# Cosformer attention with a token mixer on one core: a new order of all steps, narrow tiles for k'v and most transposes, eps on TensorE for 16 groups

## The chip, the core and the metric

The kernel runs on one core of a Trainium2 chip. The core has a matrix engine (TensorE, PE in the profile), three engines for elementwise work (VectorE or DVE, ScalarE or ACT, GpSimd or POOL) and a sync engine (SP), which here only issues DMAs. Each engine works through its own list of instructions in order and waits on semaphores where it needs another's result. The metric is the device time of one launch in microseconds, the median over runs.

## The reference

Two layers follow one another. The first is linear attention with a cosine weighting of positions, over 8 batches and 8 heads of 576 positions and 64 features; the second mixes tokens with weights that are made from the first layer's output.

```python
def phi(x, c, s):                       # c, s: cos and sin of pi/2 * pos/576
    r = np.maximum(x, 0.0)
    return np.concatenate([r * c, r * s], axis=-1)
q_p = phi(q, cos_w, sin_w); k_p = phi(k, cos_w, sin_w)
kv = einsum('bhsf,bhsd->bhfd', k_p, v);  z = sum(k_p, axis=2)
x = einsum('bhsf,bhfd->bhsd', q_p, kv) / (einsum('bhsf,bhf->bhs', q_p, z)[..., None] + 1e-06)
# x as [batch, 576, 512], heads side by side
wq = x @ w_q; wk = x @ w_k              # 512 -> 64
W_tok = einsum('bsd,btd->bst', wq, wk) / sqrt(64)
out = maximum(einsum('bst,btd->bsd', W_tok, x), 0.0) @ w_out
```

## The kernel before

The work is cut into 16 units H, each half of a batch's heads: batch H // 2, two pairs of heads. A suffix a or b on a step means the first or second pair alone. Everything is issued by one list of words, ORDER (line 26), which is walked from first to last (line 555): a word names a step, its number, after a colon its place in PSUM, and after an at sign its engine (A is ACT, V is DVE, G is POOL). Since each engine keeps the order in which it was given its instructions, this list sets the order on every engine and on SP. A scheduler does not move anything.

The steps of one unit H, in the order of its data:
- LK, LQ, LV (line 145): loads of k, q, v by SP, 128x576 f32 for each pair; five buffers of each, so a load for H waits for the steps that read H-5.
- RK, RQ (line 222, 225): relu of k and q to bf16 on any of the three engines. CV (line 229): cast of v to bf16. VS (line 232): product of the cast v with the table of cosines and sines (vtab), on DVE. VG (line 239): the same product straight from the loaded f32 v, on POOL, with no cast. Both write v2, of which there are two buffers, so H waits for KV of H-2.
- KV (line 268): k'v and z in PSUM. Wide, for units in KV_WIDE, it is 18 matmuls with 128 columns of weights and 260 streamed (line 275), half of whose output is not used; narrow it is 36 matmuls of 64x64 weights and 130 streamed (line 285). KE (line 304) copies it out.
- QT (line 290): transposes of relu(q); wide 9 of 128x128 (line 295), narrow 18 of 64x64 (line 301). QM (line 312): product with the table qtab, on DVE, from PSUM; two instructions after a wide QT, one after a narrow.
- N (line 332): numerators and denominators of group g = 2H + r, 20 matmuls. For g in EPS_PE two small matmuls with ones and split eps add eps to the denominators (line 348); for the others EP (line 354) adds it on ACT or DVE. RC (line 377) takes reciprocals, RJ (line 380) those of both groups of a unit at once. X (line 383): numerators times reciprocals, giving x, on DVE.
- XT or XR (lines 398, 409): transposes of x, ten of 128x128 or twenty of 64x64; XE (line 422) copies them out.

The steps of one batch b: WK and KW (x @ w_k and its copy), WQ and QW, KX and XK (wk' x and its copy), XA and XB (copies of 64x256 to the other half of the partitions, line 474), MX and ME (32 in all: wq times that, then the scaled relu). The steps of 36 rows of output: WO (line 504, four matmuls with w_out), OE (line 512, copy out to one of 16 output buffers), ST (line 518, the store, by SP). A store waits on SP for its OE, and what stands behind it on SP waits too; an OE waits for the store that last read its buffer. LW and CW load and cast the weights, TK to TB set up tables and constants, WU (line 544) issues matmuls on constants; its number gives how many and of which shape.

The list has no due times: what is placed ahead is issued ahead.

Of the kernel before, what the change touches and what calls it, by code (L numbers as in the profile page):

```python
# [31 lines left out]
RC6 LQ4a KX0:4 X6 RK2@A QT2:2 RC7 X7 CV5@A KV2:0 LK7a XK0@V LV4a QM2 XB0@G QW0@A XT3:6 LV4b KE2@A
RK5@A LK4a VS5a N5:0 WU5:2 LK4b N4:2 VS5b XE3@A RQ5@G LV7a EP5@V KV5:4 RC5 RC4 X5 XA0@A LV7b X4
QT5:6 KE5@A RQ4@G LQ7b MX0:0 QM5 XR2:2 ME0@A LQ7a QT4:4 XE2@A LQ6a N10:0 QM4 MX1:6 CV4@G LK7b EP10@A
ME1@A WK1:2 LV6b WQ1:3 RC10 KW1@A VS4 RK4@A LQ6b KX1:2 MX2:6 LW2 N11:4 XK1@V QW1@A ME2@A EP11@V
KV4:2 LK6b RC11 XA1@G X10 CV7a@A CV7b@G LK6a X11 MX5:6 MX4:0 KE4@A RQ7b@G LV6a RQ7a@A VS7 N8:2 N9:4
ME5@A LV8a ME4@A QT7:6 RK7@G LW3 EP8@V EP9@V RJ4 RQ6a@A XT5:0 X8 LW4 XB1@G XE5@A X9 KV7:2 LW5 RQ6b@G
QM7 LQ8b VG6b MX6:4 KE7@A XT4:0 LQ9b ME6@A MX7:2 XE4@V QT6:6 LV8b ME7@A N15:4 QM6 RK6a@A LQ8a MX3:2
N14:0 CV6a@G EP15@A RK6b@A WK2:6 LV9b ME3@A VS6a WQ2:7 LK8a KW2@A RC14 KV6:2 RC15 QW2@A LQ9a X14
CV8a@G KX2:7 LV9a KE6@A CW4@G X15 CW2@A N13:2 LK9a CW3@A CW5@V N12:0 EP13@V XR7:4 XK2@V LK8b WO8:6  # L40
RC13 XA2@A X13 EP12@A CV8b@G LK9b XE7@A WO2:7 RC12 VS8 LV11a WO7:2 CV9b@A RQ8a@G X12 OE8:0@A MX8:4
WO6:3 RQ8b@A RK8a@G LQ13a ME8@V OE7:1@A LQ11b XR6:0 RQ9a@G LQ10a WO1:6 CV9a@A XE6@V RQ9b@G LK11b
OE2:2@A WO4:2 LK11a VS9 OE6:3@A LQ11a RK8b@A QT9:0 RK9a@G OE1:4@A WK3:3 LV11b QM9 QT8:4 RK9b@G KW3@A
# [14 lines left out]
ME23@A OE20:10@V XR13:4 RQ15a@G MX22:6 RQ15b@V MX20:0 ST20 ME22@A WO15:2 VG15a ST17 XE13@V ME20@A  # L58
ST8 N28:6 OE18:9@V OE15:14@A ST9 N29:0 EP28@A QT15:4 RK15@A EP29@V RC28 WK6:3 RC29 X29 WO25:2 KW6@A
QM15 WQ6:3 OE25:15@A KV15:0 X28 QW6@A ST25 ST7 KX6:3 KE15@A ST15 N31:0 ST18 XR14:6 EP31@V N30:4 ST0  # L60
XE14@V WO23:2 EP30@A ST10 XK6@A RJ15 ST16 X30 XA6@G WO24:3 ST5 OE23:7@A XB6@G X31 WO26:2 OE24:0@A
# [537 lines left out]
```

## Time and profile before

| | before |
|---|---|
| median of 3 runs | 120.26 us (119.72 to 120.61) |
| profiled execution, first to last instruction | 117.9 us |
| granted TensorE clock, mean | 0.997 |
| moved by DMA | 39.38 MB, of it 29.62 read and 9.44 written in HBM |
| loads of k, q, v | 96 of 288 KB |
| stores | 36 of 256 KB |

The page gives the span of the profiled execution, 117.9 us; the launch and what lies around the span are in the runs' times alone, so the median stands 2.4 us above it. The page's busy time of an engine is a share of this span over stages with different limits. It is therefore read with the slices and the table of stretches, which show when an engine is full, and with the chain of waits, which shows what ended last. In the groups of instructions each row gives line, engine, operation, output and input, count, then busy time in us and the mean duration of one in ns, then idle time just ahead of them and what ended it. Durations of matmuls overlap, so busy time divided by the count is less than the mean.

### The profile page before, as it was taken

The page shows a single profiled execution, that of the slowest core. Times are in us where ns is not written, and L with a number is a line of the kernel's source. Part 1 is how long each engine was busy: PE and PEld are TensorE (multiplying, and loading weights), DVE is VectorE, ACT ScalarE, POOL GpSimd, SP SyncE. Part 2 cuts the span into 40 slices and gives each one's busy share as a digit, 9 for nine tenths or more (in the row PEclk, how much of TensorE's full clock was granted, in tenths as well). Part 3 has the DMA queues.
Part 4 walks back from the last instruction along what each step waited for, and adds up shares of the span by engine and source line. Part 5 has one row for each costly group of instructions (what it writes and reads, how often), then busy time and mean ns, then how long its engine had stood idle before and what let it go on. Part 6 is the DMA issues. An engine that isn't in the chain of part 4 may idle for free.

```text
span 117.9 us, 4967 instructions
## 1 busy us (share of the span) xinstructions
PE 96.3 (82%) x2109; PEld 65.3 (55%) x2109; DVE 91.0 (77%) x163; ACT 82.7 (70%) x146; POOL 64.8 (55%) x66
## 2 busy tenths in 40 slices
...
DMA  3999999999999999999999899786989456999874
GB/s 95 353 389 408 393 363 351 391 389 396 385 393 389 391 385 387 389 395 384 387 381 341 271 317 379 274 253 215 299 285 321 171 205 268 402 343 402 340 306 172
DMA packets 20662, 39.38 MB, mean 334 GB/s; under 512 B 3232, under 2 KB 3232, under 8 KB 20640
## 3 DMA queue, kind: packets, MB, share of 16 engines
...
HBM read 29.62 MB, written 9.44 MB: 331 GB/s over the span
## 4 chain that ended last, share of the span: by engine, by line
PE 46%; DMA 25%; DVE 9%; SPq 8%; ACT 4%; issue 3%; POOL 2%; POOLq 0%; DVEq 0%
PE ps L509 23%; DMA kraw<-in_k_dram 11%; DMA vraw<-in_v_dram 9%; SPq L145 8%; DMA qraw<-in_q_dram 5%; DVE qm L316 5%; PE ps L340 4%; PE ps L452 3%; PE ps L466 3%; PE ps L489 3%; PE ps L439 3%; PE ps L285 3%; PE ps L419 2%; PE ps L295 2%; POOL rq L205 2%
## 5 line engine op out<-in xcount | busy, mean ns | idle before, releaser
L248 POOL TENSOR_TENSOR v<-vraw,vtab 128x1152 bf16<-128x1152 f32 (+1 forms) x12 | 35.6, 2976 | 4.5 <-DVE qm L316 2.5
L509 PE MATMUL ps<-wow,mix 128*128 128x512 bf16 x144 | 34.6, 380 | 0.0
L393 DVE TENSOR_TENSOR x<-ps,rec 128x640 bf16<-128x640 f32 x32 | 25.4, 816 | 0.7
L209 ACT COPY o<-ps 128x512 f32<-128x512 f32 x25 | 14.6, 590 | 10.5 <-PE ps L509 9.2
L316 DVE TENSOR_TENSOR qm<-ps,qtab 128x1152 bf16<-128x1152 bf16 x28 | 19.7, 749 | 1.3 <-PE ps L295 1.2
L509 PEld LDWEIGHTS <-mix 128*128 128x128 bf16 x144 | 12.5, 98 | 14.5 <-issue 1.7
L295 PE MATMUL ps<-ident,rq 128*128 128x128 bf16 x126 | 10.3, 232 | 10.9 <-ACT rq L203 10.0
L234 DVE TENSOR_TENSOR v<-vb,vtab 128x2304 bf16<-128x2304 bf16 (+1 forms) x11 | 12.0, 1110 | 7.5 <-ACT vb L209 6.7
L500 ACT ACTIVATE mix<-ps 128x576 bf16<-128x576 f32 x23 | 14.5, 651 | 2.5 <-PE ps L489 2.3
L340 PE MATMUL ps<-kvs,qm 64*128 64x65 bf16 x640 | 14.0, 193 | 2.8 <-DVE qm L316 1.8
L340 PEld LDWEIGHTS <-qm 64*128 64x128 bf16 x640 | 12.6, 96 | 4.9 <-issue 3.3
L295 PEld LDWEIGHTS <-rq 128*128 128x128 bf16 x126 | 8.2, 104 | 12.5 <-issue 9.9
L203 ACT ACTIVATE rk<-kraw 128x1152 bf16<-128x1152 f32 (+1 forms) x14 | 13.9, 995 | 0.5 <-DMA kraw<-in_k_dram 0.3
L211 POOL TENSOR_SCALAR kx<-kx 64x256 bf16<-64x256 bf16 x10 | 4.0, 400 | 15.8 <-ACT kx L209 10.1
L205 POOL TENSOR_SCALAR rq<-qraw 128x576 bf16<-128x576 f32 (+1 forms) x13 | 10.1, 776 | 4.4 <-ACT rk L203 2.6
L211 POOL TENSOR_SCALAR vb<-vraw 128x576 bf16<-128x576 f32 (+1 forms) x7 | 5.7, 809 | 10.8 <-DMA vraw<-in_v_dram 9.5
L285 PE MATMUL ps<-v,rk 64*64 64x130 bf16 x432 | 9.1, 228 | 1.9 <-ACT mix L500 0.7
L209 ACT CAST kvs<-ps 128x260 bf16<-128x260 f32 (+1 forms) x15 | 6.5, 436 | 5.1 <-PE ps L285 3.8
L285 PEld LDWEIGHTS <-rk 64*64 64x64 bf16 x432 | 7.5, 112 | 4.3 <-ACT mix L500 1.3
L502 DVE TENSOR_SCALAR mix<-ps 128x576 bf16<-128x576 f32 x9 | 6.8, 753 | 3.3 <-PE ps L489 3.1
L213 DVE COPY xT<-ps 128x1280 bf16<-128x1280 bf16 (+1 forms) x9 | 7.3, 813 | 2.2 <-PE ps L419 2.0
L203 ACT ACTIVATE rq<-qraw 128x576 bf16<-128x576 f32 (+1 forms) x10 | 8.3, 830 | 0.9 <-DMA qraw<-in_q_dram 0.8
...
## 6 DMA issues: line engine op xcount, KB each, us to landing
kraw<-in_k_dram SPq DMA_DIRECT2D x32, 288.0 KB, 5.9
qraw<-in_q_dram SPq DMA_DIRECT2D x32, 288.0 KB, 5.9
vraw<-in_v_dram SPq DMA_DIRECT2D x32, 288.0 KB, 5.9
...
```

Of the source, the lines that this page charges most:

```text
L203: A.activation(dst, s, AF.Relu)
L205: eng.tensor_scalar(dst, s, FMAX, 0.0, op0=ALU.min, op1=ALU.max)
L209: A.copy(dst, s)
L234: V.tensor_mul(v2_b[H % NV2][:, part, :, :, 0:D], vb_b[H % NPREP][:, part].unsqueeze(3).to_broadcast([P, n, C, 2, D]), vtab.unsqueeze(1).t ...
L248: G.tensor_mul(dst[:, part, :, :, 0:D], s[:, part].unsqueeze(3).to_broadcast([P, n, C, 2, D]), vtab.unsqueeze(1).to_broadcast([P, n, C, 2, ...
L285: nc.tensor.matmul(kv_v[o, r, :], rk_of(H)[a, pr, c, :], v2_b[H % NV2][a, pr, c, :, 0:D + 1], start=(c == 0), stop=(c == C - 1))
L295: nc.tensor.transpose(qt_v[:, c, :], rq_b[H % NPREP][:, c, :, :], ident)
L316: V.tensor_mul(qm_b[H % NQM][:, :, r, 0:C, :], q_t[:, r].unsqueeze(1).to_broadcast([P, 2, C, H2]), qtab)
L340: nc.tensor.matmul(nv[:, pr, u, :], qm_b[H % NQM][a, s, r, 2 * u:2 * u + 2, :], kv_b[H % 2][a, r, pr if H in KV_WIDE else 0, s, 0:D + 1], ...
L393: V.tensor_tensor(x_b[b % NX][:, :, 4 * h:4 * h + 4, :].rearrange("p u (w r) d -> p r w u d", r=2)[:, r], nv[:, :, :, 0:D], rec(g).to_broa ...
L500: A.activation(dst, s, AF.Relu, scale=scale_moe)
L509: nc.tensor.matmul(o, mix_b[bp % 2][:, m, rt * P:(rt + 1) * P], wow[:, m, :], start=(m == 0), stop=(m == NDM - 1))
```

## The change

ORDER is replaced as a whole. All steps of the computation stay; on which engine they run, in what halves, and where they stand, changes throughout. Three settings change with it: all KV are narrow, all QT but those of units 0, 2 and 5 are narrow, and eps is added by TensorE in 16 groups instead of 5. Three of the four XT become XR. WU issues four matmuls at the start where one stood later. Units are taken in pairs in nearly the same sequence, but from unit 0 instead of 1.

Counts of the steps that go to an engine by choice (A, V, G as above; h is one pair of heads, f both or no halves):

| step | before | after |
|---|---|---|
| VS (V) | 6f 5h | 11h |
| VG (G) | 3f 9h | 2f 17h |
| CV | A 2f 4h, G 2f 5h | A 4h, G 4h, V 3h |
| RK | A 9f 5h, G 1f 4h, V 1f 1h | A 2f 17h, G 1f 4h, V 5h |
| RQ | A 3f 7h, G 3f 10h, V 1f 1h | A 2f 12h, G 1f 9h, V 2f 1h |
| EP | A 12, V 15 | A 5, V 11 |
| RC, RJ (V) | 24, 4 | 30, 1 |
| XE | A 7, V 9 | A 3, V 13 |
| KW | A 7, V 1 | A 3, V 5 |
| XK | A 4, V 4 | A 7, V 1 |
| XA and XB | A 6, G 10 | A 6, G 1, V 9 |
| ME | A 23, V 9 | A 28, V 4 |
| OE | A 25, V 11 | A 27, V 9 |
| CW | A 3, G 2, V 1 | G 6 |

KE, QW, X, QM, loads and stores keep their numbers and engines. The old list is cut below to its start, the part around KV11 and KV10, its last loads and its end; the new one is whole.

```diff
 ORDER = """
-LK1b TB TI LQ1a LQ0a TK LV1b TZ LV1a LK1a LQ1b TQ LQ0b LK0a RQ1a@G LV0a TW TV LV0b LK0b CV1@A LV3a
-LV3b VS1b RQ1b@A LQ3b VS1a T2 QT1:0 LQ3a RK1a@A RK1b@V RQ0@V LK3b KV1:2 QM1 LK3a QT0:4 KE1@A CV0@G
-LV2b RK0@A LW1 N2:2 VS0 N3:0 LQ2a LK2a VG3 QM0 KV0:6 LW0 KE0@A LV2a RC3 EP2@A X3 RQ3@A N0:6 N1:4
...
-WO9:5 LK12a X19 LK10b QT11:6 LQ13b OE9:7@A RQ10@G LV12b KV11:2 XA3@A QM11 XR8:0 LK12b KE11@A XR9:6
...
-KV10:2 OE3:9@V RQ12a@A QT13:6 OE12:10@A VG12 MX18:0 WO14:5 QM13 KE10@A ST12 ME18@A LK13b XR11:2
...
-RK13@A RJ12 QT14:0 X24 WO21:2 KW5@A X25 CV14a@G KV13:4 OE21:10@A QM14 CV14b@A WQ5:3 ST21 KE13@A
-KX5:2 LQ15b VS14 LQ15a XR12:4 XK5@A N27:0 ST3 XE12@A N26:6 LK15a RK14a@G WO20:2 RC26 EP27@V RC27
-XA5@G RK14b@A X27 WO19:4 XB5@G QW5@A VG15b X26 KV14:0 OE19:2@A MX21:6 KE14@A MX23:4 WO18:3 ME21@V
...
-XB7@G ST28 MX31:0 MX28:4 MX30:6 ME31@V ME28@A WO29:2 ME30@A OE27:7@V MX29:4 OE29:4@V WO30:0 ME29@A
-ST27 ST29 WO32:1 OE30:2@V WO33:4 ST30 OE32:9@V WO34:0 ST32 OE33:8@A WO35:1 ST33 OE34:7@V WO31:4 ST34
-OE35:4@A ST35 OE31:2@A ST31
+TB LV0b LQ0b LQ0a LV0a TI TQ CV0b@G LV1b LK0a LK0b WU17:0 TK TV LV1a TW CV0a@A T2 RQ0a@V LQ1a LQ1b
+TZ RK0a@A LK1b RQ0b@G LK1a CV1b@V LV2b LV2a LQ2a RQ1a@G VS0b LK2b LQ2b LK2a QT0:0 LQ3a RK0b@A CV1a@A
+LQ3b LW1 VS0a LW0 QM0 LV3a LV3b KV0:2 LK3b RQ1b@G VS1a LK3a LV4b LQ4b VG2 VS1b LQ5a KE0@A QT1:2 LQ5b
+LQ4a LV4a LK4a LV5a RK1b@A LK4b RQ3a@G LK5a QM1 N1:0 LK5b LV5b RK1a@A RC1 LW5 LW3 N0:4 RC0 KV1:6
+KE1@A LW2 CW1@G N2:6 EP2@A LW4 CW0@G RQ2a@A N3:2 X1 RQ2b@A X0 LQ6a RK2a@A LQ7b EP3@V XR0:4 RC2 LV6b
+LQ7a QT2:0 RK2b@A RC3 X3 X2 XR1:6 RQ3b@A LQ6b XE0@V KV2:4 KE2@A VG3a QM2 XE1@V LK6a LV7a LV6a CV3b@A
+VG4b QT3:2 WQ0:4 QM3 WK0:5 KW0@V RQ5@G LK6b N4:6 RK3b@A LV7b VG4a N5:2 VS3b KX0:5 XK0@A QW0@A EP5@V
+LK7a RK3a@V XA0@A RC5 RC4 X5 X4 KV3:0 MX1:4 MX0:2 KE3@A N6:0 ME0@A LK7b XR2:6 RC6 XB0@A ME1@A VG5a
+XE2@A X6 N7:2 RK5@G RC7 X7 MX3:0 RQ4@V LV8b XR3:2 QT5:6 ME3@A XE3@V QM5 LV8a CW3@G WK1:0 LQ8b KW1@A
+RK4@A LK8a QT4:2 WQ1:1 KX1:0 KV4:6 XK1@A QM4 XB1@V QW1@A CV5b@V VS5b LQ8a XA1@V KE4@A MX2:2 MX7:0
+MX6:4 N8:6 ME2@A ME6@A CW2@G ME7@A N9:2 LK8b KV5:4 LV9a KE5@A RC9 RC8 MX4:0 N11:4 X9 X8 ME4@A RC11
+N10:2 X11 LV9b CW4@G MX5:6 XR4:0 RC10 LQ9b CW5@G WO1:4 X10 ME5@A RQ7b@G CV6b@G XR5:2 RQ6a@A WO4:5
+RQ7a@G WO0:6 XE4@V LK9a LQ9a WO7:7 XE5@A LK9b VS6b QT7:2 LV10a OE4:0@V WQ2:5 RK6a@A OE1:1@A QM7
+CV6a@V VS6a RQ6b@G LV10b QT6:0 WO8:4 OE0:2@A WO2:6 RK6b@A KV6:2 QW2@A CV7b@A VG7a QM6 RK7a@V KE6@A
+OE7:3@A LV11b WK2:5 N12:2 RK7b@G VS7b N13:0 OE2:4@A KW2@A VG8b RC12 KV7:6 EP13@V LQ10a LQ10b X12
+OE8:5@A KE7@A RC13 X13 LK10b KX2:5 N14:6 N15:2 XR6:0 LV11a XK2@A RC15 XB2@A WO6:5 WO3:4 VG8a RC14
+RK8a@A RQ8@A XE6@V MX10:0 X14 QT8:6 RK8b@A VG9a X15 ME10@A LK11a LK10a KV8:2 OE3:6@A XT7:0 QM8 KE8@A
+XE7@V LK11b LQ11a VG9b MX11:2 LQ11b OE6:7@A N17:6 XA2@V N16:4 EP17@V LV13a ME11@A LV12a VG10a RQ9b@A
+RC16 LV12b WK3:0 RQ9a@A LQ13b RC17 WQ3:1 KW3@A MX8:2 X16 QT9:4 CV10b@G CV11b@G KX3:0 LQ12a X17
+RK9b@A QW3@A RK9a@V KV9:6 RK10b@G ME8@A MX9:2 LK12a XK3@A QM9 ME9@V XR8:0 KE9@A LQ13a LQ12b LK12b
+N19:6 XA3@V VG11a RC19 X19 XB3@A XE8@A WO10:4 N18:2 MX12:6 MX15:0 RC18 WO9:5 X18 VS11b LK13b XR9:2
+OE10:8@A WO12:4 XE9@V RK11b@G VS10b RQ10@A ME12@A ME15@A RQ11a@G MX13:0 OE9:9@A LV13b LK14a RK10a@V
+RK11a@A QT10:2 WK4:5 KV10:6 ME13@A KV11:0 OE12:10@A LK13a QM10 LQ15b KW4@V KE10@A N21:2 EP21@V RC21
+RQ11b@A MX14:6 VG13a QT11:4 KE11@A QM11 KX4:0 ME14@A WQ4:1 N20:6 XK4@A N22:4 ST9 X21 QW4@A N23:0
+VG12 RK13b@G RQ12a@A EP22@V WO13:2 LQ14a LV15b XB4@V RC20 EP23@V VG13b LV14a LK15b RJ11 X23 WO14:3
+LQ15a RK12a@V X22 OE13:11@A WO16:2 XR11:4 MX19:0 LV15a OE14:12@A XA4@A WO11:3 X20 OE16:13@A RQ12b@A
+XE11@V ME19@A XR10:6 MX18:4 RK12b@A ST12 RQ13@V QT12:0 ME18@A WO17:2 OE11:14@A XE10@V OE17:15@A
+WK5:4 QM12 RK13a@A QT13:6 RQ15b@G MX16:2 KV12:0 KW5@V LK14b KV13:4 ME16@A KE12@A MX17:2 QM13 N25:0
+N24:6 KE13@A EP24@V EP25@V N26:4 ME17@A RC24 KX5:2 RC25 X24 EP26@A XK5@A WQ5:3 VG15b RQ14a@A RK14a@A
+LK15a X25 RC26 LQ14b N27:6 LV14b X26 EP27@A QW5@A RC27 VG14a WO20:2 XA5@A WO5:0 OE20:9@A XR12:4
+MX21:2 RQ15a@A XB5@V X27 XE12@V ME21@A OE5:10@A XR13:6 VG15a WO15:1 XE13@V MX22:4 QT15:2 MX23:6
+ME23@V ST1 ME22@A VG14b WK6:0 WO18:4 ST10 ST14 RK15@A QM15 RK14b@A WO19:5 KW6@V ST11 ST7 RQ14b@A
+OE15:1@A OE19:8@A WO21:2 OE18:12@V OE21:14@A QT14:0 KV15:6 KV14:4 MX20:2 QM14 KE15@A KE14@V N30:6
+ST5 ST0 N31:0 EP30@V EP31@V RC30 N28:4 ME20@A ST3 RC31 WQ6:2 X30 X31 KX6:3 ST19 N29:6 QW6@A EP28@A
+WO24:2 WO23:0 EP29@A RC28 XK6@A X28 RC29 XR15:4 X29 ST2 OE24:3@A XB6@V XR14:6 XE15@V ST15 MX27:2
+ME27@A OE23:10@A ST16 ST21 XE14@V ST8 WO22:1 ST23 WO25:2 OE22:2@V XA6@V ST17 WK7:3 ST18 ST24
+OE25:6@A MX25:0 MX26:6 MX24:4 ME25@A ME24@A KW7@V WQ7:2 KX7:3 QW7@V ST13 ST6 XK7@V XA7@G XB7@V
+ME26@V WO26:4 MX31:2 WO29:5 ST25 MX29:6 ME31@A MX28:2 MX30:0 OE26:8@A ME30@A ME28@A WO27:4 ST20
+WO28:0 ME29@V ST4 WO30:1 WO34:2 ST26 OE27:4@V OE29:1@V OE28:13@V WO33:0 ST22 ST29 OE30:14@V ST28
+WO32:1 WO35:3 OE34:5@A ST30 OE35:10@A ST27 WO31:2 ST34 OE33:15@V OE31:12@A OE32:3@V ST33 ST32 ST35
+ST31
 """
...
     NRAW, NPREP, NV2, NQM, NX, NXT, NOUT = (5, 2, 2, 2, 2, 2, 16)
     XC = DM // 2
-    EPS_PE = (3, 4, 14, 16, 26)
+    EPS_PE = (0, 1, 4, 6, 7, 8, 9, 10, 11, 12, 14, 15, 16, 18, 19, 20)
     NUM_JOINT = ()
     WARM_COLS = 384
     VG_SPLIT = ()
-    QT_WIDE = (0, 1, 2, 3, 4, 5, 6, 7, 8, 9, 10, 11, 12, 14)
-    KV_WIDE = (2, 4, 5, 7)
+    QT_WIDE = (0, 2, 5)
+    KV_WIDE = ()
```

29 lines of the change are left out of this document (removed).

## The prediction

> **What bounds the kernel now.** I read the page first, then a table of stretches, the chain of waits and the order of the queues.
>
> ```profile
> span 117.9 us, 4967 instructions
> PE 96.3 (82%) x2109; PEld 65.3 (55%) x2109; DVE 91.0 (77%) x163; ACT 82.7 (70%) x146; POOL 64.8 (55%) x66
> ...
> DMA  3999999999999999999999899786989456999874
> GB/s 95 353 389 408 393 363 351 391 389 396 385 393 389 391 385 387 389 395 384 387 381 341 271 317 379 274 253 215 299 285 321 171 205 268 402 343 402 340 306 172
> ```
>
> Two engines are about equally full, and the transfers are full for the first half of the span. So no single share decides; the stretches do. The next fence is the table of stretches (length; busy time of PE, PEld, DVE, ACT, POOL; granted clock; DMA share; GB/s), cut at three points: the first DVE work on data, the issue of the last matmuls of KV10, and the end of PE.
>
> ```profile
> 8.60:64.50 55.90, 48.24 (x1136) 36.59 (x1140) 50.92 (x92) 43.72 (x78) 35.31 (x30) 1.00 1.05 385
> 64.50:74.20 9.70, 8.81 (x222) 5.97 (x223) 7.98 (x13) 7.65 (x16) 6.48 (x6) 1.00 0.96 325
> 74.20:97.40 23.20, 22.39 (x568) 14.28 (x566) 20.38 (x36) 18.44 (x34) 17.40 (x9) 1.00 0.75 249
> 97.40:114.30 16.90, 16.86 (x196) 8.48 (x196) 10.87 (x18) 7.68 (x15) 1.60 (x4) 1.00 0.91 347
> ```
>
> Up to 64.5 us DVE is the fullest engine (50.92 of 55.9, 91%) and transfers run at their limit. From 74.2 us on PE is the bound: 22.39 + 16.86 = 39.25 of 40.1 us. The chain of waits says the same of the end, and the timeline of PE gives two marks, the last matmuls of KV10 and of KV15 (the last pair of heads):
>
> ```profile
> 108.98 5.30 PE ps L509 x24
> ...
> 73.52 0.72 PE L285 MATMUL ps<-v,rk 64*64 64x130 bf16 x36
> 96.67 0.72 PE L285 MATMUL ps<-v,rk 64*64 64x130 bf16 x36
> ```
>
> So I cut the change at the point where KV10 and KV11 are both done (74.2 us now). Before it, DVE's list sets the time; behind it, PE's list does. Both lists can be counted off the two orders.
>
> **The first part: DVE's list up to KV10 and KV11.** Prices are the groups of instructions (count, busy us, mean ns of one):
>
> ```profile
> L393 DVE TENSOR_TENSOR x<-ps,rec 128x640 bf16<-128x640 f32 x32 | 25.4, 816 | 0.7
> L316 DVE TENSOR_TENSOR qm<-ps,qtab 128x1152 bf16<-128x1152 bf16 x28 | 19.7, 749 | 1.3 <-PE ps L295 1.2
> L320 DVE TENSOR_TENSOR qm<-ps,qtab 128x2304 bf16<-128x2304 bf16 x2 | 2.7, 1353 | 0.3 <-PE ps L301 0.3
> L234 DVE TENSOR_TENSOR v<-vb,vtab 128x2304 bf16<-128x2304 bf16 x6 | 8.4, 1406 | 0.7 <-POOL vb L211 0.7
> L234 DVE TENSOR_TENSOR v<-vb,vtab 128x1152 bf16<-128x1152 bf16 x5 | 3.6, 754 | 6.8 <-ACT vb L209 6.7
> L213 DVE COPY xT<-ps 128x1280 bf16<-128x1280 bf16 x8 | 6.6, 820 | 2.1 <-PE ps L419 2.0
> L502 DVE TENSOR_SCALAR mix<-ps 128x576 bf16<-128x576 f32 x9 | 6.8, 753 | 3.3 <-PE ps L489 3.1
> L213 DVE CAST kx<-ps 128x256 bf16<-128x256 f32 x4 | 1.7, 417 | 0.3 <-PE ps L466 0.3
> L359 DVE TENSOR_SCALAR rec<-ps 128x10 f32<-128x10 f32 x15 | 2.0, 152 | 1.6 <-PE ps L340 1.4 <-ACT rec L357 0.2
> L205 DVE TENSOR_SCALAR rk<-kraw 128x576 bf16<-128x576 f32 x1 | 0.5, 455 | 0.0
> ```
>
> Where instructions overlap I use busy time over count. Steps ahead of the mark, before and after:
> - X, 22 to 20: 2 x 25.4/32 = -1.6.
> - QM, 12 wide (two instructions each, 2 x 19.7/28 = 1.41) to 3 wide and 7 narrow (1.35): 16.9 to 13.7, -3.2. Nearly all of it is that two heads fewer are needed by then; the narrow form itself saves only 0.06 each.
> - VS (product of v on DVE), 5 full and 5 half to 11 half: 5 x 1.40 + 5 x 0.72 = 10.6 to 7.9, -2.7. The six halves that go are VG on POOL now.
> - ME on DVE 4 to 1, -2.3; XK 4 to 0, -1.7; the addition of eps (EP) 9 to 4, -0.8, as TensorE does it for 15 of the groups ahead of the mark.
> - Added: XE 4 to 7, +2.5. Three casts of v at 0.455, +1.4. RK and RQ: from one full RK, one half RK and one full RQ to four half RK, one full and one half RQ: a full one less, four halves more, +1.0 (full taken as 0.8, under two halves). XA and XB, 0 to 4: no row on DVE; between 0 and the 0.417 of the kx cast, whose rows are as long; I take the middle, 0.2, +0.8.
>
> Sum: -1.6 - 3.2 - 2.7 - 2.3 - 1.7 - 0.8 + 2.5 + 1.4 + 1.0 + 0.8 = -6.6. DVE was busy 50.92 + 7.98 = 58.9 of the 65.6 us of these two stretches, but 9% of its time goes in small waits that come with every step, so I take -6.6 as it stands and not more.
>
> **PE in that part** falls too, which is why PE does not become its bound:
>
> ```profile
> L295 PE MATMUL ps<-ident,rq 128*128 128x128 bf16 x126 | 10.3, 232 | 10.9 <-ACT rq L203 10.0
> L301 PE MATMUL ps<-ident,rq 64*128 64x64 bf16 x36 | 0.9, 190 | 0.0
> L275 PE MATMUL ps<-v,rk 64*128 64x260 bf16 x72 | 4.8, 271 | 1.0 <-ACT rk L203 0.4 <-DVE x L393 0.3 <-ACT wq L209 0.2
> L285 PE MATMUL ps<-v,rk 64*64 64x130 bf16 x432 | 9.1, 228 | 1.9 <-ACT mix L500 0.7 <-DVE qm L316 0.4 <-POOL v L248 0.4
> L348 PE MATMUL ps<-epsr,ones 64*128 64x5 bf16 x10 | 1.0, 170 | 0.0
> ```
>
> A QT costs 10.3/14 = 0.74 wide and 0.9/2 = 0.45 narrow; eleven change: -3.2. A KV costs 4.8/4 = 1.20 wide, 9.1/12 = 0.76 narrow; four change: -1.8. Eleven more groups with eps at 1.0/5 = 0.2: +2.2. Three XT become XR, of the same kind as the step from wide to narrow QT: a small gain more that I leave out. Net -2.8 over the kernel, but most of it is early, where DVE and the loads set the time. Behind the mark only three of the eleven QT and none of the KV stand; that is why I don't count it as a gain by itself.
>
> **The loads.** SP issues loads and stores in one order, and a store waits there for its copy:
>
> ```profile
> 70.36 0.33 SPq L145 DMA_DIRECT2D vraw<-in_v_dram  x1
> 75.15 0.34 SPq L519 DMA_DIRECT2D out_dram<-o  x1
> ...
> 88.87 0.43 SPq L145 DMA_DIRECT2D kraw<-in_k_dram  x1
> ...
> kraw<-in_k_dram SPq DMA_DIRECT2D x32, 288.0 KB, 5.9
> ```
>
> Between 70.7 and 75.15 nothing was issued: the store of ST12 waited, and loads stood behind it. The new order has two stores (ST9, ST12) ahead of the last load instead of seven, and both of their copies are placed far ahead. DVE had 82% in 64.5 to 74.2 against 91% before; at 91% those 9.7 us would be 8.8. I take that as the worth of freer loads: -0.9 (bounds: 0, and the whole gap of 4.5). Do the loads come early enough? The last load of heads 10 and 11 is the 72nd of its kind, with 22.5 MB up to it; at 385 GB/s from about 3.6 us (an estimate from the slow first slice) that lands at 62, four us before I need it. All loads with both stores are 30.2 MB, landing at 82.
>
> **The second part: PE's list behind KV10 and KV11.** Before it held 23 WO, 16 MX, 10 N, 3 WQ, 3 KX, 4 QT; after it holds 25 WO, 17 MX, 12 N, 4 WQ, 4 KX, 5 narrow QT; WK, XR, KV and eps are equal. Prices:
>
> ```profile
> L509 PE MATMUL ps<-wow,mix 128*128 128x512 bf16 x144 | 34.6, 380 | 0.0
> L340 PE MATMUL ps<-kvs,qm 64*128 64x65 bf16 x640 | 14.0, 193 | 2.8 <-DVE qm L316 1.8 <-ACT kvs L209 1.0
> L489 PE MATMUL ps<-wq,kx 64*128 64x288 bf16 x64 | 7.9, 286 | 0.1
> L452 PE MATMUL ps<-xT,wqw 128*64 128x288 bf16 x64 | 5.5, 292 | 0.0
> ```
>
> WO is 34.6/36 = 0.96 by busy time, but 5.30/6 = 0.88 from one to the next in the chain; I use that ratio (0.92) for all. 2 WO +1.77; N 2 x 0.44, MX 0.25, WQ 0.69 and KX (ten matmuls of 256 columns, taken like WQ) 0.69: 2.51 x 0.92 = +2.3; QT 2 x 0.74 + 2 x 0.45 to 5 x 0.45: -0.1. Sum +4.0, and all of it is on the path, as PE had 0.85 us of idle time in these 40.1.
>
> **The sum.** -6.6 - 0.9 + 4.0 = -3.5, so the span goes from 117.9 to 114.4. The start I cost at 0: the first products of v need a cast of half the size now, but their table stands behind a cast on POOL; half a microsecond either way. Those 2.4 us that the median (120.26) lies above this span are launch and end, and stay: 116.8.
>
> **POOL** gets most of what DVE and ACT lose:
>
> ```profile
> L248 POOL TENSOR_TENSOR v<-vraw,vtab 128x1152 bf16<-128x1152 f32 x9 | 21.9, 2433 | 3.0 <-DVE qm L316 2.5 <-DMA vraw<-in_v_dram 0.4
> L248 POOL TENSOR_TENSOR v<-vraw,vtab 128x2304 bf16<-128x2304 f32 x3 | 13.8, 4604 | 1.5 <-PE ps L348 1.1 <-PE ps L285 0.4
> L205 POOL TENSOR_SCALAR rq<-qraw 128x576 bf16<-128x576 f32 x10 | 6.6, 665 | 1.2 <-DMA qraw<-in_q_dram 0.7 <-PE ps L509 0.2
> ```
>
> VG goes from 9 half and 3 full to 17 half and 2 full: 8 x 2.433 - 4.604 = +14.9; less casts, RQ and XA/XB there. It is covered only as long as POOL keeps pace: with two buffers of v2, VG of head H waits for KV of head H-2. From KV10/KV11 to KV14/KV15 the list of POOL is VG13a, VG12, VG13b, VG15b, VG14a, VG15a, VG14b and two relus: 6 x 2.433 + 4.604 + 2 x 0.665 = 20.5 us. By my sum that stretch goes from 66.7 (74.2 - 7.5) to about 92 us (97.4 - 7.5, with less than half of the +4.0 ahead of it), 25 us, so POOL has 4.5 us left. If the rest becomes faster, this is what is late next.
>
> **The rivals.**
> 1. *Larger gain.* DVE's idle time up to 74.2 us is 65.6 - 58.9 = 6.7 us. If freer loads, eps without a step of its own and shorter narrow transposes take half of it, that is -3.3: 113.5. Speaks for it: several of its waits are for QT, N and loads. Against: POOL's 20.5 us then binds. I give it 0.2.
> 2. *Slower: DVE and POOL stand in each other's way.* The trace shows it:
>
> ```profile
> 86.69 1.35 DVE L234 TENSOR_TENSOR v<-vb,vtab 128x2304 bf16<-128x2304 bf16 x1
> 87.09 1.46 POOL L205 TENSOR_SCALAR rk<-kraw 128x576 bf16<-128x576 f32 x1 [2.90 <-DMA kraw<-in_k_dram]
> ```
>
> A relu of 0.67 on POOL took 1.46 beside a product on DVE, and ended half a microsecond after it. The new order has 31 DVE steps from SBUF to SBUF (11 VS, 3 CV, 5 RK, 3 RQ, 9 XA/XB) instead of 16, and 51 us of half and full products on POOL (17 x 2.433 + 2 x 4.604). If POOL's products fall on half of the 15 more, and each costs half a product, 1.2 us, that is 9.0 us; the order sets most of them into POOL's gaps, though a step that runs late misses its gap. It decides once it costs 4.7 us (four meetings): I price it at 5.8, 122.6, with 0.16. The Trainium skill (SBUF — State Buffer, section "Who interferes with whom") has it as a rule: a DVE instruction with two SBUF inputs, or in a two-port mode, and a GpSimd instruction that reads SBUF exclude each other for a whole instruction. By that rule the trace agrees (1.46 beside 1.35), and a DVE step could lose a whole 2.4 us rather than half.
> 3. *No change: the stores come late.* 34 of 36 stores now stand behind the last load, 8.9 MB; at 372 GB/s, the mean of slices 35 to 38, 24 us. If the last load lands at 82 they end by 106, hidden. Now it is issued at 88.87 and lands 5.9 later; if that stays, they end at 118.8, which is 121.2. It decides from a landing at 90 on (90 + 24 is the span I forecast); for one at 93 it gives 119.4, and that is this rival's time. All 16 output buffers are taken by then, so ACT would wait too (OE15 for ST1). Chance 0.18: loads were late for stores ahead of them, and these go.
>
> **How the numbers follow.** Forecast 0.46, with its own range 115 to 118.5 (the bounds of the loads' worth and of the start); rival 1 0.2; rival 3 0.18; rival 2 0.16. Faster by over 1%, about what a measurement of this kernel can tell from no change, is under 119.06: 0.66; within 1% 0.18; slower 0.16. The range runs from 112.8 (rival 1 and a little) to 120.8: it leaves out rival 2 and the outer end of rival 1.
>
> **What would show it.** KV10 and KV11 both done by 66.7 us (now 74.2) and the last KV of heads 14 and 15 by about 92 (now 97.4); DVE still near 91% till then; PE without gaps behind it, ending near 111; the last load issued by 77 and DMA full till about 82; no gap over 1 us on SP ahead of that. VS, CV or RK on DVE that take over 2 us, or POOL relus over 1 us, would show rival 2; OE copies that wait for stores rival 3. If KV10 and KV11 are not earlier than 71, the first step, DVE as the bound of the first part, is wrong.

## The result, and the profile after

The changed kernel takes 138.82 us (median of 4 runs, 137.52 to 140.11) against 120.16 us for the kernel before, measured beside it: a ratio of 1.152, 95% interval 1.145 to 1.159. The forecast was 116.8 with a range of 112.8 to 120.8. The change is slower by 15%, so sign and size are both missed. The medians here and below take in all runs of a kernel; one of the four of the change, 140.11, was in a slower state, and without it the median is 138.45, so the gains below may each be 0.4 us smaller. Line numbers of the changed kernel are one higher than before from L146 on (product of v on DVE L235, on GpSimd L249, N L341, WO L510).

The first fence is from the changed kernel's page: span, busy time by engine, granted clock and DMA share in 40 slices, and the shares of the chain of waits.

```profile
span 137.4 us, 5403 instructions
...
PE 100.7 (73%) x2322; PEld 65.8 (48%) x2335; DVE 104.2 (76%) x164; ACT 77.8 (57%) x145; POOL 71.7 (52%) x62
...
PEclk9999999869998569986999999997799999999997
DMA  4999999999999999997499379991300517369993
...
PE 48%; DVE 26%; issue 11%; DMA 5%; ACT 3%; SPq 2%; POOL 2%; DVEq 0%
```

DVE has one instruction more than before and is busy 13.2 us longer (104.2 against 91.0). DVE's share of the chain grew from 9% to 26%; this is that line of the kernel before:

```profile
PE 46%; DMA 25%; DVE 9%; SPq 8%; ACT 4%; issue 3%; POOL 2%; POOLq 0%; DVEq 0%
```

The granted clock, full in every stretch before, drops in several slices. The marks of the prediction stand on these rows: the matmuls of KV10 and KV11, those of KV14 and KV15, the last WO, and then the two stretches that the first and the last of them cut (length; busy time of PE, PEld, DVE, ACT, POOL; clock; DMA share; GB/s).

```profile
81.17 1.24 PE L286 MATMUL ps<-v,rk 64*64 64x130 bf16 x72
...
112.11 1.25 PE L286 MATMUL ps<-v,rk 64*64 64x130 bf16 x72
...
126.03 7.08 PE L510 MATMUL ps<-wow,mix 128*128 128x512 bf16 x32
```

```profile
8.60:82.40 73.80, 54.19 (x1458) 38.07 (x1464) 61.67 (x91) 43.47 (x80) 46.67 (x33) 0.91 0.96 342
82.40:133.10 50.70, 43.96 (x858) 26.40 (x862) 40.16 (x66) 29.02 (x57) 20.28 (x10) 0.97 0.59 217
```

KV10 and KV11 are done at 82.4 us (before 74.2, forecast 66.7), the last KV at 113.4 (before 97.4, forecast 92) and PE at 133.1 (before 114.3, forecast 111). So 8.2 us are lost in the first part and 10.6 in the second (50.7 against 40.1). PE is busy for 54.19 of 73.8 us in the first and 43.96 of 50.7 in the second: it is full again only behind the last KV, and up to there waits cost the time. The trace shows two kinds of them.

**DVE waits for GpSimd.** These are the groups of DVE that grew (count, busy us, mean ns of one):

```profile
L235 DVE TENSOR_TENSOR v<-vb,vtab 128x1152 bf16<-128x1152 bf16 x11 | 11.5, 1064 | 0.1
L214 DVE COPY kx<-kx 64x256 bf16<-64x256 bf16 x9 | 7.8, 867 | 0.4
L206 DVE TENSOR_SCALAR rk<-kraw 128x576 bf16<-128x576 f32 x5 | 6.5, 1306 | 0.0
L206 DVE TENSOR_SCALAR rq<-qraw 128x1152 bf16<-128x1152 f32 x2 | 2.5, 1250 | 0.0
```

A half VS took 0.754 before and takes 1.064 now, a half RK 0.455 and now 1.306. A free copy of kx takes 0.22, as the next fence shows, and the mean is 0.867. Single instructions say why: the first three rows are from DVE's timeline, the two below from that of GpSimd, beside the third and then beside the second.

```profile
37.27 0.22 DVE L214 COPY kx<-kx 64x256 bf16<-64x256 bf16 x1
...
55.62 2.44 DVE L206 TENSOR_SCALAR rk<-kraw 128x576 bf16<-128x576 f32 x1
...
86.51 3.03 DVE L214 COPY kx<-kx 64x256 bf16<-64x256 bf16 x1
```

```profile
82.57 6.89 POOL L249 TENSOR_TENSOR v<-vraw,vtab 128x1152 bf16<-128x1152 f32 x2 [5.25 <-issue]
```

```profile
55.37 4.91 POOL L249 TENSOR_TENSOR v<-vraw,vtab 128x1152 bf16<-128x1152 f32 x2 [9.31 <-PE ps L286]
```

The copy that starts at 86.51 ends at 89.54, and the two products on GpSimd end at 89.46: a step of a fifth of a microsecond lasted until GpSimd was done, and everything queued behind it on DVE was late by 2.8 us. The whole trace has the same pattern. Of the 31 steps from SBUF to SBUF on DVE, 11 have no GpSimd instruction beside them and take their free time; 16 take longer, and each of these ends a fixed time behind a GpSimd instruction that ran beside it: the copies of kx 0.08 to 0.09 us, RK and the cast 0.31 to 0.32, VS and RQ 0.60 to 0.62. The other four lose nothing. In ten of the 16 that instruction is a product, in six a relu or a cast. Over the four groups and the casts of v the excess is 11 x 0.310 + 9 x 0.647 + 5 x 0.851 + 2 x 0.495 + 3 x 0.150 = 14.9 us (the casts took 605 ns each), more than the whole growth of DVE; all of it lies in those 16 steps.

**PE waits for nothing that the profile names.** The timeline of PE has stalls put down to "issue", which the kernel before has none of over 0.35 us; three of the five here that are longer than that:

```profile
25.90 0.33 PE L341 MATMUL ps<-kvs,qm 64*128 64x65 bf16 x10 [1.83 <-issue]
...
44.08 0.66 PE L420 MATMUL ps<-ident,x 64*128 64x64 bf16 x18 [1.68 <-issue]
...
83.86 0.36 PE L302 MATMUL ps<-ident,rq 64*128 64x64 bf16 x13 [0.58 <-issue]
```

The five together (also 0.37 and 0.48) are 4.9 us. Each falls in the middle of a step, between two matmuls of the same kind, whose inputs were there. Counted in PE's program, a weight load and a matmul being two rows, they stand 66 to 72 rows ahead of the 2nd, 3rd, 6th, 12th and 17th multiple of 256. That is the size of a block of the instruction queue in part 3 of the page:

```profile
q8 instruction: 18, 0.29, 0.9%
```

18 transfers of 16 KB, for a PE program of some 2 x 2335 = 4670 rows (4218 before): one for some 260 rows. The trace also times these transfers. The second runs from 23.22 to 24.26 us, here in the queues of the window from 23.2 to 24.3:

```profile
q8 instruction: 1, 0.02, 5.9%
```

The stall at the third multiple of 256 ends at 25.90, 1.64 us behind it. So it is at each of the five: the transfer whose number is one less than the multiple ends 1.2 to 1.7 us before the stall does. PE waited for its own instructions. The traces of the runs below have 29 more stalls over 0.35 us that are put down to "issue"; all stand 62 to 72 rows ahead of a multiple of 256 (counted by weight loads), and all end 1.2 to 1.6 us behind that transfer.

The stalls are also followed by a lower clock. The first two rows are stretches of 8 us around the first two stalls of the fence above (the clock is the number ahead of the last two):

```profile
24.00:32.00 8.00, 4.74 (x132) 3.48 (x126) 5.67 (x12) 4.04 (x8) 7.33 (x5) 0.79 1.05 391
...
40.00:48.00 8.00, 5.57 (x117) 3.11 (x108) 5.71 (x11) 2.90 (x5) 3.76 (x4) 0.72 1.05 377
...
58.00:66.00 8.00, 5.25 (x116) 3.76 (x118) 6.39 (x11) 2.94 (x6) 6.00 (x3) 0.79 0.80 288
90.00:98.00 8.00, 4.14 (x69) 2.38 (x71) 7.50 (x9) 2.96 (x6) 2.42 (x2) 0.79 0.40 149
```

The last two rows have no such stall: there PE waited 2.59 and 4.29 us for DVE. So the clock falls with a long wait of PE of either kind.

### The profile page after: what moved, and what is told of

The parts are those of the page before. It is cut to its first block, busy times and chain, and to the rows that moved or that the text cites. A ratio compares the mean times of both kernels' runs of the same rounds, so it can differ in the third digit from the quotient of the medians.

```text
span 137.4 us, 5403 instructions
## 1 busy us (share of the span) xinstructions
PE 100.7 (73%) x2322; PEld 65.8 (48%) x2335; DVE 104.2 (76%) x164; ACT 77.8 (57%) x145; POOL 71.7 (52%) x62
## 4 chain that ended last, share of the span: by engine, by line
PE 48%; DVE 26%; issue 11%; DMA 5%; ACT 3%; SPq 2%; POOL 2%; DVEq 0%
PE ps L510 20%; DVE x L394 7%; PE ps L286 6%; PE ps L341 5%; DMA qraw<-in_q_dram 5%; DVE qm L321 4%; PE ps L420 4%; DVE v L235 3%; PE ps L490 3%; DVE rk L206 3%; PE ps L440 3%; DVE xT L214 3%; PE ps L302 2%; SPq L146 2%; PE ps L467 2%
## 5 line engine op out<-in xcount | busy, mean ns | idle before, releaser
L249 POOL TENSOR_TENSOR v<-vraw,vtab 128x1152 bf16<-128x1152 f32 (+1 forms) x19 | 49.3, 2613 | 22.5 <-PE ps L286 9.3
L510 PE MATMUL ps<-wow,mix 128*128 128x512 bf16 x131 | 36.2, 407 | 1.3 <-issue 0.6
L321 DVE TENSOR_TENSOR qm<-ps,qtab 128x2304 bf16<-128x2304 bf16 x13 | 17.6, 1352 | 5.3 <-PE ps L302 5.2
L510 PEld LDWEIGHTS <-mix 128*128 128x128 bf16 x144 | 13.3, 102 | 16.3 <-issue 3.9
L341 PE MATMUL ps<-kvs,qm 64*128 64x65 bf16 x640 | 15.0, 197 | 3.2 <-issue 2.3
L341 PEld LDWEIGHTS <-qm 64*128 64x128 bf16 x640 | 13.0, 98 | 6.3 <-issue 5.7
L204 ACT ACTIVATE rk<-kraw 128x576 bf16<-128x576 f32 (+1 forms) x19 | 13.7, 731 | 1.3 <-DMA kraw<-in_k_dram 1.1
L420 PE MATMUL ps<-ident,x 64*128 64x64 bf16 x300 | 7.9, 200 | 7.8 <-DVE x L394 5.8
L210 ACT CAST kvs<-ps 128x260 bf16<-128x260 f32 x15 | 5.7, 377 | 13.2 <-PE ps L286 13.2
L420 PEld LDWEIGHTS <-x 64*128 64x128 bf16 x300 | 6.2, 100 | 12.0 <-DVE x L394 7.3
L235 DVE TENSOR_TENSOR v<-vb,vtab 128x1152 bf16<-128x1152 bf16 x11 | 11.5, 1064 | 0.1
L490 PE MATMUL ps<-wq,kx 64*128 64x288 bf16 x64 | 8.4, 301 | 2.2 <-DVE x L394 2.2
L214 DVE COPY o<-ps 128x512 f32<-128x512 f32 x9 | 5.9, 686 | 4.0 <-PE ps L510 4.0
L302 PE MATMUL ps<-ident,rq 64*128 64x64 bf16 x234 | 6.3, 198 | 3.4 <-POOL rq L206 2.1
```

The costliest lines, as they stand in the source:

```text
L204: A.activation(dst, s, AF.Relu)
L210: A.copy(dst, s)
L214: V.tensor_copy(dst, s)
L235: V.tensor_mul(v2_b[H % NV2][:, part, :, :, 0:D], vb_b[H % NPREP][:, part].unsqueeze(3).to_broadcast([P, n, C, 2, D]), vtab.unsqueeze(1).t ...
L249: G.tensor_mul(dst[:, part, :, :, 0:D], s[:, part].unsqueeze(3).to_broadcast([P, n, C, 2, D]), vtab.unsqueeze(1).to_broadcast([P, n, C, 2, ...
L321: V.tensor_mul(qm_b[H % NQM][:, :, :, 0:C, :].rearrange("p s r c d -> p s r (c d)"), qt_view(place["QT", H]).unsqueeze(1).to_broadcast([P, ...
```

## The experiments

Two theories stood at the start. **L**: DVE's steps from SBUF to SBUF wait for products on GpSimd, and that is the loss. **F**: narrow tiles double the instructions of QT and KV, and PE waits for blocks of its own program. In the orders below, the letter behind @ is the engine (V is DVE, A is ACT, G is GpSimd).

**1. The new order with the old wide tiles** (takes away most of F).

```diff
-    QT_WIDE = (0, 2, 5)
-    KV_WIDE = ()
+    QT_WIDE = (0, 1, 2, 3, 4, 5, 6, 7, 8, 9, 10, 11, 12, 14)
+    KV_WIDE = (2, 4, 5, 7)
```

> The new order with the old wide tiles (14 wide QT, 4 wide KV); nothing else changes. Theory L (DVE steps from SBUF to SBUF wait for POOL's products): nothing of that changes, and PE gets 4.4 us of work more, so 138 to 142 us; DVE's copies of kx still near 0.87 us. Theory F (PE's instruction list is fetched in blocks of 256 and narrow tiles use it up faster than blocks come): PE loses 342 instructions, the six stalls at block ends (5.3 us in all) shrink to under 2 us, and with them the stretches at half clock that follow: 130 to 134 us.

Measured 136.81 us (ratio 1.139, 1.133 to 1.145). The stalls on "issue" shrink to this, among PE's waits (us in total, times, longest), and it brings 2.0 us only:

```profile
PE ps L341 <- issue: 0.7, 1, 0.7
PE ps L420 <- issue: 0.6, 1, 0.6
```

The time lies between the two ranges that were expected, above that of F and below that of L. So F is real but is not the main loss as the kernel stands: where PE no longer waits for instructions, it waits for others instead (for DVE's RK, 3.2 us in all against 1.7).

**2. The new order with twenty small DVE steps on ACT** (takes away most of L; every RK, RQ, CV, XA and XB that was on DVE).

```diff
-CV6a@V VS6a RQ6b@G LV10b QT6:0 ... RK7a@V KE6@A
+CV6a@A VS6a RQ6b@G LV10b QT6:0 ... RK7a@A KE6@A
...
-XE7@V ... XA2@V N16:4 EP17@V
+XE7@V ... XA2@A N16:4 EP17@V
```

> The new order, with the 20 casts, relus and kx copies of DVE (CV, RK, RQ, XA, XB) put on ACT at the same places in the list; VS stays on DVE, VG on POOL. Theory L: DVE loses 6.9 us of work and some 12 us of waiting, ACT gains 11 us; 125 to 130 us, and DVE busy falls from 104 to about 85. Theory F: DVE's waits cost little of the time, 135 us or more. If ACT becomes the bound instead, it would be over 90% busy in stretches of 8 us and the time would not fall below 134.

Measured 130.54 us (1.088, 1.080 to 1.096): 8.3 us less than the change, and 0.5 above the range that L gave. The two stretches, cut at its own KV10 and KV11 (78.7) and its own end of PE:

```profile
8.60:78.70 70.10, 54.90 (x1465) 39.27 (x1470) 49.69 (x79) 49.99 (x95) 45.35 (x33) 0.93 0.99 360
78.70:124.10 45.40, 42.91 (x854) 25.84 (x861) 33.10 (x58) 32.51 (x64) 20.33 (x10) 1.00 0.68 247
```

3.7 us came back in the first part and 5.3 in the second. The stalls on "issue" do not go (5.2 us in all over 0.35). Two stand at the same matmuls of the unchanged PE program, the 11th of the N at 26 us (10 left) and, shrunk to 0.17, the 3rd of the XR at 44 us (18 left), though all of DVE's work around them moved; the one of 2.10 is new.

```profile
25.98 0.33 PE L341 MATMUL ps<-kvs,qm 64*128 64x65 bf16 x10 [1.42 <-issue]
44.56 0.44 PE L420 MATMUL ps<-ident,x 64*128 64x64 bf16 x18 [0.17 <-issue]
58.22 0.40 PE L341 MATMUL ps<-kvs,qm 64*128 64x65 bf16 x14 [2.10 <-issue]
```

**3. Both**: the orders of run 2 and the tile lists of run 1.

> Both edits at once. Theory L alone: as e2, at most 3 us slower for PE's extra work (126 to 133). Theory F alone: as e1. If both hold and each stall also costs a stretch at half clock: 118 to 124 us. If the order itself is what costs, for instance POOL's chain of products through two buffers of v2, it stays over 126.

Measured 125.85 us (1.046, 1.039 to 1.053). Wide tiles are worth 4.7 us here (130.54 to 125.85), against 2.0 in run 1: once DVE is not late, the blocks of instructions are what PE waits for (this run has no stall over 0.35 on "issue", where run 2 has 5.2 us of them). The two losses hide each other, and together they are 13.0 of the 18.7 us. The time is above the 118 to 124 that was expected if both hold, so something else costs too. For the other 5.7 the stretches of this kernel are to be held against those of before:

```profile
8.60:64.50 55.90, 45.65 (x1071) 34.59 (x1074) 43.46 (x74) 40.83 (x77) 39.84 (x27) 0.97 1.06 387
64.50:74.60 10.10, 9.28 (x253) 6.22 (x253) 8.21 (x13) 10.01 (x20) 6.62 (x7) 1.00 0.97 346
74.60:119.40 44.80, 43.41 (x827) 26.43 (x835) 33.29 (x61) 32.41 (x64) 20.32 (x10) 1.00 0.69 250
```

KV10 and KV11 are done at 74.6 (74.2 before) although up to then DVE was busy for 51.67 us (58.90 before), PE for 54.93 (57.05) and ACT for 50.84 (51.37). PE's part behind them is 44.8 us (40.1 before). The rest, 0.7, is the end behind PE (4.3 against 3.6). The chain of waits seems to say what held the first part; these are its shares, and pieces of it in order of time:

```profile
DMA 47%; PE 31%; ACT 7%; DVE 6%; SPq 3%; issue 2%; ACTq 0%; DVEq 0%
```

```profile
4.67 6.79 DMA qraw<-in_q_dram
11.48 6.01 DMA qraw<-in_q_dram
...
53.66 5.89 DMA vraw<-in_v_dram
59.62 3.62 DMA vraw<-in_v_dram
63.28 0.67 ACT rq L204
```

From 4.67 to 63.24 us this chain is transfers alone, ten in a row, each beginning as the one before ends (the dots leave out six). But its last link does not hold. The load of v that is issued at 59.62 lands at 65.56 by the trace, behind the start of the relu of q that it is said to release, and ACT's timeline has that relu as the second of two that follow each other, with no wait ahead:

```profile
62.70 1.25 ACT L204 ACTIVATE rq<-qraw 128x576 bf16<-128x576 f32 x2
```

So the loads, at 387 GB/s here and 385 before, are not shown to set this part. Nor does DVE's list set it alone, which is 7.2 us shorter without moving the mark, nor the sum of any one engine's work. The last load of units 10 and 11 lands at 63.3; the 11.3 us from there to the mark are steps of ACT, DVE and PE that wait for each other, with ACT busy for 10.01 of the last 10.10.

**4. Six products of v from GpSimd back to DVE**, in the changed kernel and in run 3.

```diff
-VG8b ... VG8a ... VG9a ... VG9b ... VG14a ... VG14b
+CV8b@A VS8b ... CV8a@A VS8a ... CV9a@A VS9a ... CV9b@A VS9b ... CV14a@A VS14a ... CV14b@A VS14b
```

> The new order with six half products of v put back from POOL to ACT and DVE (VG of units 8, 9 and 14 become a cast on ACT and VS on DVE, at the same places); so 13 half and 2 full products on POOL, as much as the old order has. If POOL's added products are what blocks DVE (14.6 us less of POOL time): DVE's waits beside them fall by 4 us or more and the time by 4 to 7, to 132 to 135 us. If it is the added DVE steps that make the meetings, whichever products stay: 137 to 140 us, for the six VS are 4.3 us of DVE work more and meet POOL too.

Measured 136.24 us (1.129, 1.122 to 1.136): 2.6 us less, for six products fewer to wait for and six more DVE steps that can wait. That lies between the two ranges; DVE's excess over free durations, counted as above, falls from 14.9 to 9.4 us.

> e3 (wide tiles, the 20 DVE steps on ACT) with the same six half products back on ACT and DVE. What is left of DVE's waits in e3 is in VS alone (2.7 us). If POOL's chain of products is what still costs 5.6 us against the old order: 120 to 123.5 us. If what is left is the order of the second part, which holds 4 us of PE work more behind KV10 and KV11: 125 to 127 us.

Measured 128.68 us (1.067, 1.061 to 1.073): 2.8 us more than run 3 and above both ranges. With the small steps off DVE the products on GpSimd are better left there; with those steps on DVE, six products fewer help. So it is the meeting of the two that costs, not the number of products by itself.

**5. The old order with the new narrow tiles** (F alone, in a kernel with few waits of kind L): the two lists of run 1 the other way round, in the kernel before.

> The old order with the new narrow tiles (QT narrow but for units 0, 2 and 5, all KV narrow); nothing else changes. By the prediction's prices PE loses 3.2 + 1.8 = 5.0 us of work, mostly early where DVE sets the time: 118.5 to 120 us. Theory F: the old order is also fed by blocks, so stalls at block ends appear in the stretch up to 50 us and it is slower: 121 to 126 us. Theory L says nothing of it (120).

Measured 123.14 us (1.020, 1.011 to 1.030). The tiles that the change was costed to gain 5.0 us of PE work with (3.2 for QT, 1.8 for KV) make the old kernel 2% slower, as F expected. PE stalls inside steps, here in two QT, where the kernel before has no such stall:

```profile
26.14 0.27 PE L295 MATMUL ps<-ident,rq 128*128 128x128 bf16 x2 [0.84 <-issue]
31.88 0.62 PE L295 MATMUL ps<-ident,rq 128*128 128x128 bf16 x8 [1.39 <-issue]
```

These two QT are still wide; a third stall, 1.47 us at 90.10, falls in a narrow one. It is not the narrow form of a transpose that waits, but whichever instruction stands there when a block is late. The trace is of the longest of the four runs, 125.80 us, so how much of the 2% these stalls are is not shown.

**6. The old order with eps by PE, and with late narrow tiles.** The first moves eps of 13 more groups to PE and drops their steps on DVE and ACT; the second makes QT10, QT12 and QT14 narrow, which come when transfers are less dense.

```diff
-    EPS_PE = (3, 4, 14, 16, 26)
+    EPS_PE = (0, 1, 3, 4, 6, 7, 8, 9, 10, 11, 12, 14, 15, 16, 18, 19, 20, 26)
```

> The old order with eps added by TensorE in 18 groups (the 16 of the new kernel and the two more that the old one has), EP left out for them; RJ of units 4 and 10 becomes two RC. ACT loses about 2 us, DVE 0.9, PE gains 2.6 of busy time and 52 instructions. By the prediction's prices 119.3 to 120.3 us. If the blocks of PE's instructions bind, the added ones give it back: 120.3 to 121.5 us.

Measured 121.52 us (1.007, 1.003 to 1.011): no gain (0.7% slower), and one stall on "issue" of 2.2 us, 66 rows ahead of the 7th multiple of 256.

```diff
-    QT_WIDE = (0, 1, 2, 3, 4, 5, 6, 7, 8, 9, 10, 11, 12, 14)
+    QT_WIDE = (0, 1, 2, 3, 4, 5, 6, 7, 8, 9, 11)
```

> The old order with QT narrow in units 10, 12 and 14 alone, which lie in the stretch from 74 us on, where PE is the bound and transfers are not at their limit. PE loses 3 x 0.29 = 0.9 us of busy time there and gains 54 instructions. If narrow tiles only cost where blocks of instructions come slowly, that is at full transfers: 119.2 to 120.0 us. If they cost anywhere: 120.4 us or more.

Measured 121.38 us (1.003, 0.999 to 1.007): not to be told from no change.

**7. 48 tiny matmuls more in the first idle time of PE**, which move the whole program 96 rows down and give no other engine any work.

```diff
     def WU(i, ps, eng):
...
+        for _ in range(48):
+            nc.tensor.matmul(bank(ps)[0:cols, 0:8], wc[0:rows, WARM_COLS:WARM_COLS + cols],
+                             wc[0:rows, 0:8], start=True, stop=True)
```

> The changed kernel with 48 tiny matmuls more in the first idle time of PE (64x64 weights, 8 columns), while PE waits 4.24 us for the first rq: 96 rows more in PE's program, no work for anything else. Theory F (PE waits for the next block of 256 of its instructions): the block ends stay at the same rows, so the stalls that stood at 25.90 and 44.08 move 48 matmuls up the list, the first from the 11th matmul of the second half of an N to the 5th of the 20 matmuls of WK1 (L440), the second from the 3rd of 20 XR matmuls to the first of an N; the one in QT11 at 83.86 goes into the 72 matmuls of KV10 and KV11. Time 136 to 141. Rival (the stall belongs to those instructions or to what they read): it stays at the 11th of that N and the 3rd of that XR, at 25.9 and 44.1.

Measured 137.37 us (1.139, 1.132 to 1.146), 1% less than the change. The stalls at the 11th matmul of that N and in the XR at 44 us are gone, so the rival falls. All that are left of 0.4 us and more:

```profile
74.58 0.20 PE L341 MATMUL ps<-kvs,qm 64*128 64x65 bf16 x2 [0.48 <-issue]
...
84.48 0.37 PE L341 MATMUL ps<-kvs,qm 64*128 64x65 bf16 x13 [0.71 <-issue]
...
101.58 0.37 PE L341 MATMUL ps<-kvs,qm 64*128 64x65 bf16 x13 [0.67 <-issue]
```

All three stand where the program as it now is has 70 to 72 rows to go to a multiple of 256, the 11th, 13th and 15th; by the old rows they would be somewhere inside blocks. But the stalls that were named, in WK1, at the start of an N and in KV10 and KV11, did not come: those blocks were there in time. So the program's rows say where a stall can be, and not whether there is one; which blocks came late had changed altogether. In the changed kernel the ends at 20.22 and 25.90 us lie 5.7 us apart, about what a load takes to land there (5.9). That the fetches wait behind the loads is a reading that fits these two; no run here separates it, and the stall at 114.89 came with the DMA engines 30% busy in the 4 us ahead of it. And again the time hardly moved: 3.0 us of these stalls went (4.9 to 1.9) and the time fell by half of that. For the first of them a wait for DVE took its place, as this row shows (DVE's RK was late by 2.44, where this KV waited 0.31 for it in the changed kernel).

```profile
27.65 0.72 PE L286 MATMUL ps<-v,rk 64*64 64x130 bf16 x36 [2.44 <-DVE rk L206]
```

**8. Run 2 in two halves**: only the nine copies of kx to ACT, and only the eleven relus and casts.

> The changed kernel with only the nine small copies (XA, XB; 64x256, bf16, SBUF to SBUF) moved from DVE to ACT. They cost DVE 7.8 us where 2.0 were expected, so theory L (each waits for the end of a product on GpSimd) takes about 5.8 us of busy time away and expects 3 to 5 us less: 134 to 136. Rival (DVE is not what the other engines wait for): under 1.5 us less, 137.3 to 139.

Measured 131.37 us (1.090, 1.086 to 1.094): 7.5 us less.

> The changed kernel with only the eleven relus and casts (RK, RQ, CV; float32 to bf16) moved from DVE to ACT, the small copies left on DVE. They waited for some 6.1 us of DVE time in all, against the 5.8 of the copies. Theory L: 3 to 5 us less, 134 to 136, and with the nine copies (8.3 us together in the run that moved all twenty) the two parts add up. Rival: the loss is not additive, since what one step no longer waits for the next one does: the two parts sum to clearly less than 8.3, or to more.

Measured 132.60 us (1.101, 1.096 to 1.106). The halves give 7.5 and 6.2 us, 13.7 in sum, and both together 8.3. Each is worth more than was expected, and they are far from additive: that with either half gone the other's waits mostly no longer stand on the path is the reading that fits. They have not gone from DVE itself, as the rows of the first of the two kernels show, where the RK that stayed wait as long as ever:

```profile
L235 DVE TENSOR_TENSOR v<-vb,vtab 128x1152 bf16<-128x1152 bf16 x11 | 11.2, 1034 | 0.1
...
L206 DVE TENSOR_SCALAR rk<-kraw 128x576 bf16<-128x576 f32 x5 | 6.7, 1340 | 0.0
```

Nine copies that take 0.22 us each when free, 2.0 us in all, cost the kernel 7.5 us of time, so it is their waits and not their work that was saved.

No kernel of these beats the one before.

## Why the prediction was wrong, point by point

- **"Before it, DVE's list sets the time"; "-6.6".** This is the step that failed, twice. The list did not get shorter: where 6.6 us were to come off 58.9, DVE was busy for 61.67 us up to the mark, which came 8.2 us later instead of 7.5 earlier; the next two points say why. And a shorter list alone does not move the mark: run 3 takes off 7.2 us, about what was forecast, with PE and ACT no busier than before, and KV10 and KV11 are done at 74.6 instead of 74.2. That the change missed 71 does not tell these two apart; run 3 does. The evidence for the step was a share, DVE's 91% of the stretch, while DVE had 9% of the chain of that kernel. The freer loads, -0.9, are lost in the same way. The landing of the loads of heads 10 and 11, forecast "at 62, four us before I need it", held (63.0 us in the change, 63.3 in run 3); what does not fit into four us is the work behind it, which takes 11.3 in run 3 and 19.4 in the change.
- **The prices of DVE's steps.** A free duration was taken for each. "XA and XB ... I take the middle, 0.2" is right for a free copy (0.22) and a quarter of the mean (0.867), and the nine copies were worth 7.5 us. RK at 0.455 took 1.306, a half VS at 0.72 (0.754 as a mean) took 1.064. The term of XA and XB, +0.8, should have carried the wait for GpSimd, an example of which stood in the prediction.
- **Rival 2, "DVE and POOL stand in each other's way"** was the mechanism that decided, with 0.16 of the chance and a price of 5.8 us. It assumed that products fall on half of the 15 steps more, at 1.2 us each, 9.0 us, and that the order avoids some. Measured, 16 of all 31 steps wait, by 0.93 us on average, 14.9 us in all, VS that were there before among them, and taking twenty steps off DVE gave 8.3 us of time. So the share and the size of a meeting were about right; that the old steps meet GpSimd too, and its relus and casts as well as its products, was left out. The Trainium skill (SBUF — State Buffer, "Who interferes with whom") was cited there for a loss of a whole GpSimd instruction rather than half. The trace agrees: each of the 16 ends a fixed time behind the GpSimd instruction, and the worst, a copy of 0.22, took 3.03.
- **PE, "net -2.8 ... I don't count it as a gain by itself".** Not even that is safe: the narrow tiles cost 2.0 us in the new order as it is, 4.7 once DVE is not late, and 2% in the old one. No rival had it. The number that would have warned can be counted from the two lists: some 450 rows more in PE's program (2 x 2335 against 2 x 2109). The Trainium skill (Runtime: NRT & Kernel Launch, "Instruction fetch mechanics") says that instructions come in blocks of 256 by a DMA queue of their own, and that the cost is mostly hidden. The blocks and the queue agree with the 18 transfers and with the places and ends of the stalls; "hidden" does not hold for PE here, which stalled for 4.9 us.
- **The second part, +4.0.** About right: 44.8 against 40.1 us in run 3 is +4.7, and three QT (11, 12 and 14) are wide there that were costed narrow (3 x 0.29 = 0.9 of work). In the change itself it was +10.6, the other 5.9 being waits of the first kind (5.3) and the blocks (0.6).
- **POOL "is covered".** With the small steps off DVE it is: giving six products back in run 3 made it 2.8 us slower. What was not asked is what GpSimd's being busy does to others.
- **Rival 1, a larger gain,** did not come: DVE's waits grew instead. **Rival 3, late stores,** did not decide: the end behind PE grew from 3.6 to 4.3 us only.

In sum: 138.8 less 8.3 (waits of DVE for GpSimd) less 4.7 (blocks of instructions) is 125.8, and the 5.7 from there to the kernel before are the longer list of PE in the second part, 4.7, with 0.4 at the mark and 0.7 at the end. What stays open is which of the steps behind the last load hold the first part at 74.6 us in run 3, where ACT, DVE and PE wait for each other, and what the waits of VS (866 to 1095 ns on average in these runs, 754 before) cost by themselves: no kernel without them was tried.
